# Nine key chunks for two heads, gate products between transposes and masks, and later expert weights, in a fused attention and expert kernel

## The chip, the cores and the metric

The kernel runs on one core of one Trainium2 chip. A core has five engines with queues of their own: TensorE (PE in the profile; its weight loads are listed apart as PEld), VectorE (DVE), ScalarE (ACT), GpSimd (POOL) and SyncE (SP), which here starts nearly all transfers. The metric is the device time of one execution in microseconds, as the median of several runs. Before the change it is 995.38 us (three runs, 995.27 to 997.89).

## The reference

Two stages. The first is attention with a top-32 mask in 64 pairs of batch and head, each with 576 queries and keys of 64 elements. The second sends every token to its best of eight experts, and each expert keeps only its 80 tokens of highest gate.

```python
# q, k, v: (8, 8, 576, 64); w_gate (512, 8); w1 (8, 512, 1024); w2 (8, 1024, 512); capacity 80
scores = scale * q @ k.T
kth = np.partition(scores, -32, axis=-1)[..., -32:-31]
attn = softmax of scores where scores >= kth, else 0          # row sums + 1e-9
x = (attn @ v) as (4608, 512)                                 # heads side by side

logits = x @ w_gate
expert_idx, gate_w = argmax and its softmax probability
for e in range(8):
    tok_idx = the tokens of e, at most the 80 with the largest gate_w
    out[tok_idx] = gate_w[tok_idx, None] * (np.maximum(x[tok_idx] @ w1[e], 0) @ w2[e])
# all other rows of out are 0
```

## The kernel before

The attention works on 32 head pairs n. Each has five tiles t of 128 queries: four with both heads, and a short one that holds the last 64 queries of both heads on one tile. A unit is one tile of one head (the short tile is one unit), so a pair has nine units, 288 in all, and one step of the program's loop brings one new unit into a software pipeline. For a unit, VectorE finds the 32nd largest score: MAX8 over six pieces of 96 columns, three rounds over the 48 candidates, a count of how many scores exceed a pivot (ScalarE, `sign`), and a last MAX8 over `y`, the scores multiplied by their signs.

```python
for j in range(NG):                                # 6 pieces
    nc.vector.max(out=cand[:, j, :], in_=s[:, j * S // NG : (j + 1) * S // NG])      # L241
# ... cut: three rounds of max and match_replace on cand (L252, L260)
nc.scalar.activation(sign, s, Act.Sign, bias=w9[:, 7:8], scale=-1.0, accum_out=cnt)  # L257
engine = nc.gpsimd if i in self.odd else nc.vector
engine.tensor_tensor(out=y, in0=s, in1=sign, op=Alu.mult)                            # L264
nc.vector.max(out=w9[:, 8:], in_=y)                                                  # L266
# ... cut: pick writes the threshold thr[:, i] (L269)
```

Then the scores that fall below the threshold are masked. `below` makes a mask per unit: 1 on GpSimd (even units), or the distance below the threshold on ScalarE (odd units). `turn_w` transposes the scores by chunks of 128 keys on TensorE, and adds the transposed mask with a large negative factor in the same PSUM accumulation, so that exp makes it 0. 576 keys are four chunks and a half, and each head takes five: the last one starts 64 keys early, so it overlaps the fourth, and its first 64 rows meet zeros in v.

```python
def turn_w(self, n, t):
    # ... cut: ab holds 2 heads x 4 chunks in PSUM, cc the last chunks, the products with v and the sums
    keys = [slice(c * P, c * P + P) for c in range(NF)] + [slice(S - P, S)]
    dst = [[ab[:, h, c, :] for c in range(NF)] + [cc[:, h * P : (h + 1) * P]] for h in range(g)]
    for h in range(g):
        sc = self.s.pop(i + h)
        for c in range(NK):                                                          # L316
            nc.tensor.matmul(dst[h][c], lhsT=sc[:, keys[c]], rhs=ident, ..., is_transpose=True)
    for h in range(g):
        mk = self.mask.pop(i + h)
        for c in (NF, *range(NF)):                                                   # L321
            nc.tensor.matmul(dst[h][c], lhsT=mk[:, keys[c]], rhs=huge if i + h in self.odd else minus, ...)
    nc.scalar.activation(wT[:, 2 * NF : ...], cc[:, : g * P], Act.Exp, scale=scale / TINY)   # L323
    nc.scalar.activation(wT[:, : g * NF, :], ab..., Act.Exp, scale=scale / TINY)             # L325
```

`back` multiplies these weights with v and a column of ones (L336, forty half-width products a full tile), `over` takes the reciprocal of the sums on VectorE (L348), `divide` scales on ScalarE (L359). When a pair is done, `norm` stores it, transposes it (L201), copies it as xT (L376), multiplies it with the gate's weights (L381) and copies the product (`part`, L388), each part in some later step:

```python
def norm(...):
    # ... cut: store xn
    yield 1
    ps = self.four()...; self.turn_in(ps, xn, cs); nc.scalar.copy(xT[:, at], ps[:, at])
    yield 1
    lp = self.four()...                   # the one PSUM buffer that front and turn use too
    for c in cs:
        for r in range(0, P, TL):
            nc.tensor.matmul(lp[r : r + TL, c, :], lhsT=xT[...], rhs=wg[:, hp, :], start=True, stop=True)
    nc.scalar.copy(part, lp[:, cs])
    yield 0
    # ... cut: VectorE adds part to lg (L392); after every eighth pair the gates
```

A part that ends before `yield 1` takes a step in which no `front` is due, since both need the one buffer. `front` (L226) makes the scores of the tile four units ahead, and ScalarE copies them to SBUF (L233).

Of the 4.2 MB of weights of each expert, four experts' are loaded during the attention. The fifth's are loaded when the attention's buffers are free, and those of experts 5 to 7 as the first ones' buffers come free. In the last stage the routing finds the kept tokens (mostly VectorE), GpSimd gathers their rows by an indirect transfer, and TensorE computes the experts.

```python
def finish(wpool, full):
    late = stack.enter_context(tc.tile_pool(name="late", bufs=1))
    for dma in load_w(4, late):
        dma()
    # ... cut: routing, gathers, hidden(e), product(e), store(e); load_w(e + 4, wpool) for 5 to 7
wpool = main.enter_context(tc.tile_pool(name="wpool", bufs=4))
for e in range(4):
    slow += load_w(e, wpool, 4)          # issued one by one in the attention's steps
```

Of the kernel before, what the change touches and what calls it, by code (L numbers as in the profile page):

```python
# [22 lines left out]
HUGE = 2.0 ** 100  # L23
TINY = 2.0 ** -48
# [3 lines left out]
def kernel(  # L28
# [120 lines left out]
    class Attention:  # L149


        def __init__(self, stack, lean):
# [6 lines left out]
            self.s, self.top, self.cnt, self.y, self.mask, self.w, self.xn = ({} for _ in range(7))  # L159
            self.thr, self.z = thr_all, z_all  # L160
# [4 lines left out]
            for j in range(1 if lean else 3):  # L165
                t = vpool.tile([P, NK, 2, D + 1], F32, name=f"vb{j}")
                nc.gpsimd.memset(t[:, :, :, D : D + 1], 1.0)
                nc.gpsimd.memset(t[: P - TL, NF, :, :], 0.0)
                self.vb.append(t)
# [4 lines left out]
        def load(self, n, b, hp):  # L174
            one = bass.ds(b, 1)
            tiles = []
            for name, src in (("qn", q), ("kn", k)):
# [7 lines left out]
                tiles.append(t)  # L185
            t = self.vb[n % len(self.vb)]
            for h in range(2):
                nc.sync.dma_start(
                    t[:, :NF, h, :D], v[one, 2 * hp + h, : NF * P, :].rearrange("o (c p) d -> p (o c) d", p=P))
            nc.sync.dma_start(  # L190
                t[P - TL :, NF, :, :D], v[one, 2 * hp : 2 * hp + 2, NF * P :, :].rearrange("o h p d -> p (o h) d"))
            self.qk[n] = tiles
# [23 lines left out]
        def front(self, n, t):  # L216
# [11 lines left out]
            s = self.rows.tile([P, 2 * S], F32, name="s", tag="s", bufs=2 if self.lean else 5)  # L228
            for h in range(g):
                self.s[i + h] = s[:, h * S : (h + 1) * S]  # L230
# [41 lines left out]

        def below(self, i):

            self.top.pop(i)
            self.mask[i] = self.rows.tile([P, S], BF16, name="mask", tag="mask", bufs=3)
            if i in self.odd:
                nc.scalar.activation(self.mask[i], self.s[i], Act.Relu, bias=self.thr[:, i : i + 1], scale=-1.0)  # L278
                return
            nc.gpsimd.tensor_scalar(self.mask[i], self.s[i], self.thr[:, i : i + 1], None, op0=Alu.is_lt)  # L280
# [13 lines left out]
        def drop(self, i):  # L294

            s, top = self.s[i], self.top.pop(i)
            self.mask[i] = self.rows.tile([P, S], BF16, name="mask", tag="mask", bufs=2)
            nc.vector.tensor_scalar(self.mask[i], s, self.thr[:, i : i + 1], top[:, 0, 0:1], op0=Alu.is_lt, op1=Alu.add)

        def turn_w(self, n, t):  # L300
# [9 lines left out]
            keys = [slice(c * P, c * P + P) for c in range(NF)] + [slice(S - P, S)]  # L310
            dst = [[ab[:, h, c, :] for c in range(NF)] + [cc[:, h * P : (h + 1) * P]] for h in range(g)]

            for h in range(g):
                sc = self.s.pop(i + h)
                for c in range(NK):
                    nc.tensor.matmul(dst[h][c], lhsT=sc[:, keys[c]], rhs=ident, start=c == 0 or (c == NF and h == 0), stop=False,  # L316
                                     is_transpose=True, skip_group_check=True)
            for h in range(g):
                mk = self.mask.pop(i + h)
                for c in (NF, *range(NF)):  # L320
                    nc.tensor.matmul(dst[h][c], lhsT=mk[:, keys[c]], rhs=huge if i + h in self.odd else minus, start=False, stop=True, skip_group_check=True)  # L321
            wT = self.rows.tile([P, 2 * NK, P], F32, name="wT", tag="wT")
            nc.scalar.activation(wT[:, 2 * NF : 2 * NF + g, :].rearrange("p h r -> p (h r)"), cc[:, : g * P], Act.Exp,  # L323
                                 scale=scale / TINY)
# [590 lines left out]
```

## Time and profile before

| | before |
|---|---|
| median of three runs | 995.38 us |
| span of the profiled execution | 993.1 us |
| attention, to the last gate sums | about 870 us |
| routing, gathers and experts | about 124 us |
| ScalarE busy, GpSimd busy | 797.2 us, 451.9 us |
| HBM read, written | 63.19 MB, 20.19 MB |
| two head pairs in mid-attention (the products with v at 365.47 and 417.64 us) | 52.17 us |

Engine rows give busy time, share of the span and number of instructions. The slices are fortieths of the span, 24.8 us each, with the busy share in tenths. A group line names its line of the program, the engine and operation, what is written and read with shapes, the number of instructions, and then busy us and mean ns of one, followed by the engine's idle time just before them and what ended it. Durations of neighbouring matmuls overlap in such a mean. A line of the waits says who waited for whom: us in total, how many times, and the longest.

### The profile page before, as it was taken

To read this page: it belongs to the slowest core of one execution; us is meant where nothing else is said; L and a number is where in the kernel's file an instruction comes from. 1 tells how busy PE (TensorE), PEld (TensorE's weight loads), DVE (VectorE), ACT (ScalarE), POOL (GpSimd) and SP (SyncE) were. 2 spreads that over 40 slices of the span, in tenths; PEclk is the share of its full clock that TensorE was granted. 3 is DMA by queue.
4 is the path that set the end of the run, shared out by engine and by line. 5 is a ranking of instruction groups with operands and counts; after the bars stand their busy time and mean duration, and the time that the engine had idled before them with its cause. 6 is when DMAs were issued, how large, how long until landed. Compare 5 with 4: busy or idle time off the path is not lost.

```text
span 993.1 us, 35590 instructions
## 1 busy us (share of the span) xinstructions
PE 885.5 (89%) x13368; PEld 704.9 (71%) x13368; DVE 870.6 (88%) x5072; ACT 797.2 (80%) x1652; POOL 451.9 (46%) x330
## 2 busy tenths in 40 slices
PE   5899999998989989899899999999899898679996
PEld 3677777776767777677677777777677676668896
DVE  5899999999999999999999999999999999571110
ACT  3899999999999989999999999999899999601110
POOL 2445555555455545554555555555455555302111
PEclk9999999999999999999999999999999999979998
DMA  3344453333332323333333322222222100044920
GB/s 72 97 126 131 129 134 92 92 92 92 91 79 62 87 82 86 92 92 93 88 82 83 91 49 51 50 50 50 50 50 49 41 23 14 16 170 142 382 76 28
DMA packets 167893, 85.76 MB, mean 86 GB/s; under 512 B 117792, under 2 KB 154656, under 8 KB 167712
## 3 DMA queue, kind: packets, MB, share of 16 engines
q1 hardware_dynamic: 166688, 80.78, 29.7%
q0 software_dynamic: 1024, 2.62, 0.9%
q8 instruction: 107, 1.75, 0.7%
q14 instruction: 74, 0.61, 0.2%
HBM read 63.19 MB, written 20.19 MB: 84 GB/s over the span
## 4 chain that ended last, share of the span: by engine, by line
DVE 53%; PE 24%; ACT 18%; issue 5%; DMA 1%; POOL 0%; POOLq 0%; SPq 0%; ACTq 0%; DVEq 0%
DVE cand L241 17%; DVE w L266 12%; DVE cand L260 6%; DVE y L264 6%; ACT s L233 4%; DVE top L252 4%; PE yp L799 4%; ACT wT L325 3%; PE sp L201 3%; PE cc L336 3%; ACT sign L257 3%; DVE pick L269 3%; ACT mask L278 2%; PE sp L226 2%; PE ab L316 2%
## 5 line engine op out<-in xcount | busy, mean ns | idle before, releaser
L241 DVE MAX8 cand<-s 128x8 f32<-128x96 f32 x1728 | 393.9, 250 | 8.9 <-ACT s L233 8.8
L280 POOL TENSOR_SCALAR mask<-s,thr_all 128x576 bf16<-128x576 f32 x144 | 248.2, 1723 | 144.9 <-DVE pick L269 121.8
L264 POOL TENSOR_TENSOR y<-s,sign 128x576 f32<-128x576 f32 x144 | 184.8, 1283 | 277.3 <-DVE pick L269 128.0
L336 PEld LDWEIGHTS cc<-vb,wT 128*64 128x64 f32 x5760 | 181.7, 138 | 111.2 <-ACT wT L325 98.5
L257 ACT ACTIVATE sign<-s,w 128x576 bf16<-128x576 f32 x288 | 225.4, 783 | 22.8 <-DVE w L252 22.2
L336 PE MATMUL cc<-vb,wT 128*64 128x65 f32 x5760 | 204.0, 225 | 40.6 <-ACT wT L325 38.9
L266 DVE MAX8 w<-y 128x8 f32<-128x576 f32 x288 | 217.8, 756 | 2.5 <-POOL y L264 2.5
L226 PE MATMUL sp<-both 64*128 64x288 f32 (+1 forms) x1280 | 202.1, 435 | 15.0 <-ACT part L388 6.5
L233 ACT ACTIVATE s<-sp 128x1152 f32<-128x1152 f32 (+1 forms) x161 | 167.3, 1040 | 12.7 <-PE sp L226 11.9
L316 PE MATMUL ab<-ident,s 128*128 128x128 f32 x1148 | 175.6, 282 | 0.0
L325 ACT ACTIVATE wT<-ab 128x1024 f32<-128x1024 f32 (+1 forms) x159 | 148.8, 936 | 0.0
L226 PEld LDWEIGHTS sp<-both 64*128 64x128 f32 (+1 forms) x1280 | 105.6, 179 | 53.8 <-ACT part L388 8.5
L316 PEld LDWEIGHTS ab<-ident,s 128*128 128x128 f32 x1148 | 127.5, 141 | 11.6 <-issue 0.9
L321 PEld LDWEIGHTS <-mask 128*128 128x128 bf16 x1440 | 92.1, 98 | 42.4 <-ACT mask L278 19.6
L252 DVE MAX8 top<-cand 128x8 f32<-128x48 f32 x576 | 116.9, 203 | 0.0
L260 DVE MATCH_REPLACE8 cand<-top,cand 128x48 f32<-128x48 f32 x576 | 112.9, 196 | 0.0
L278 ACT ACTIVATE mask<-s,thr_all 128x576 bf16<-128x576 f32 x144 | 112.3, 780 | 0.4
L264 DVE TENSOR_TENSOR y<-s,sign 128x576 f32<-128x576 f32 x144 | 107.6, 747 | 4.5 <-ACT sign L257 4.5
L359 ACT ACTIVATE xn<-cc,z_all 128x64 f32<-128x64 f32 (+1 forms) x320 | 86.5, 318 | 1.4 <-DVE z_all L348 0.8
L316 PE MATMUL cc<-ident,s 128*128 128x128 f32 x288 | 78.9, 274 | 0.3 <-ACT xn L359 0.2
L269 DVE SCALAR_TENSOR_TENSOR pick<-past,cnt,w 128x9 f32<-128x9 f32 x288 | 69.5, 241 | 0.2 <-DVE z_all L348 0.2
L323 ACT ACTIVATE wT<-cc 128x256 f32<-128x256 f32 (+1 forms) x160 | 56.2, 351 | 12.0 <-PE cc L321 11.3
(188 smaller groups left out, 965.7 us busy)
## 6 DMA issues: line engine op xcount, KB each, us to landing
w<-in_moe_w_dram SPq DMA_DIRECT2D x32, 512.0 KB, 4.7
w<-in_moe_w_dram SPq DMA_DIRECT2D x8, 2048.0 KB, 9.8
out_dram<-zero SPq DMA_DIRECT2D x9, 1024.0 KB, 6.3
qn<-in_q_dram SPq DMA_DIRECT2D x64, 128.0 KB, 2.6
kn<-in_k_dram SPq DMA_DIRECT2D x64, 128.0 KB, 2.5
vb<-in_v_dram SPq DMA_DIRECT2D x64, 128.0 KB, 2.6
xd<-xn SPq DMA_DIRECT2D x32, 256.0 KB, 4.3
qn<-in_q_dram SPq DMA_DIRECT2D x32, 32.0 KB, 2.5
```

The lines of the kernel that those rows point to most:

```text
L226: nc.tensor.matmul(o, lhsT=qT[d, t * P : t * P + m], rhs=kT[d, j * HS : (j + 1) * HS], start=True, stop=True)
L233: nc.scalar.activation(s[:, j * HS : (j + w) * HS].rearrange("p (j c) -> p j c", c=HS), ps[:, j : j + w, :HS], Act.Copy, scale=TINY)
L241: nc.vector.max(out=cand[:, j, :], in_=s[:, j * S // NG : (j + 1) * S // NG])
L252: nc.vector.max(out=dst, in_=cand)
L257: nc.scalar.activation(sign, s, Act.Sign, bias=w9[:, 7:8], scale=-1.0, accum_out=cnt)
L260: nc.vector.match_replace(out=cand, in_to_replace=dst, in_values=cand, imm_value=LOW)
L264: engine.tensor_tensor(out=y, in0=s, in1=sign, op=Alu.mult)
L266: nc.vector.max(out=w9[:, 8:], in_=y)
L280: nc.gpsimd.tensor_scalar(self.mask[i], self.s[i], self.thr[:, i : i + 1], None, op0=Alu.is_lt)
L316: nc.tensor.matmul(dst[h][c], lhsT=sc[:, keys[c]], rhs=ident, start=c == 0 or (c == NF and h == 0), stop=False, is_transpose=True, skip_gr ...
L325: nc.scalar.activation(wT[:, : g * NF, :], ab.rearrange("p h c r -> p (h c) r")[:, : g * NF, :], Act.Exp, scale=scale / TINY)
L336: nc.tensor.matmul(cc[r : r + TL, o], lhsT=wT[:, h * NF + c if c < NF else 2 * NF + h, r : r + TL], rhs=vb[:, c, h if t < NF else r // TL, ...
```

## The change

A tile's two heads lie side by side, 1152 score columns in all, which are exactly nine chunks of 128. The change transposes and masks these nine, where each head had five; the middle chunk holds the last 64 keys of head 0 and the first 64 of head 1. For that, v is laid out anew: four chunks of head 0, four of head 1 that start at its key 64, four of head 1 from its key 0 (for the short tile, which still has five chunks), and four single chunks padded with zeros. Head 1's v is so loaded twice. The mask of both heads lies in one tile, and one factor (`huge`, now 2^80) serves both kinds of mask, since a chunk may hold both.

```diff
-                t = vpool.tile([P, NK, 2, D + 1], F32, name=f"vb{j}")
+                t = vpool.tile([P, 3 * NF + 4, D + 1], F32, name=f"vb{j}")
...
+        def load_v(self, n, b, hp):
+            for j, h, k0 in ((0, 0, 0), (1, 1, TL), (2, 1, 0)):
+                nc.sync.dma_start(t[:, j * NF : (j + 1) * NF, :D], v[one, 2 * hp + h, k0 : k0 + NF * P, :]...)
+            # ... two loads of 64 rows, one of 64 rows of both heads; called one unit pair after load
...
-            self.mask[i] = self.rows.tile([P, S], BF16, name="mask", tag="mask", bufs=3)
+                self.mask[n, u // 2] = self.rows.tile([P, 2 * S], BF16, name="mask", tag="mask", bufs=2 if self.lean else 3)
...
-        def turn_w(self, n, t):
+        def turn_w(self, n, t, between=None):
...
+            keys = [slice(c * P, c * P + P) for c in range(2 * NF + 1)] if t < NF else [...]
+            for c, o in enumerate(dst):
+                nc.tensor.matmul(o, lhsT=sc[:, keys[c]], rhs=ident, ..., is_transpose=True)
+            if between:
+                between()
+            for c in sorted(range(len(dst)), key=lambda c: c != NF):
+                nc.tensor.matmul(dst[c], lhsT=mk[:, keys[c]], rhs=minus if self.lean else huge, ...)
+            wT = self.rows.tile([P, 2 * NF + 1, P], F32, name="wT", tag="wT")
+            nc.scalar.activation(wT[:, 2 * NF, :], cc[:, :P], Act.Exp, scale=scale / TINY)
```

The gate's products of a pair no longer wait for a step without a front. They go into the next tile's `turn_w`, after its transposes and before its masks, where TensorE may have to wait for the masks:

```diff
             nc.scalar.copy(xT[:, at], ps[:, at])
-            yield 1
+            yield 2
...
+                def gate():
+                    for g in later:
+                        if ready[g] == 2:
+                            ready[g] = next(g)
...
-                    self.turn_w(*units[i - 4][:2])
+                    self.turn_w(*units[i - 4][:2], gate)
...
-                    if ready[g] and busy and not last:
+                    if (ready[g] == 1 and busy or ready[g] == 2 and i < NU + 4) and not last:
```

The larger v and mask tiles need room. Three experts' weights are loaded during the attention and not four, and those of experts 3 and 4 at the start of the last stage:

```diff
-        late = stack.enter_context(tc.tile_pool(name="late", bufs=1))
-        for dma in load_w(4, late):
-            dma()
+        late = stack.enter_context(tc.tile_pool(name="late", bufs=2))
+        for e in (3, 4):
+            for dma in load_w(e, late):
+                dma()
...
-        wpool = main.enter_context(tc.tile_pool(name="wpool", bufs=4))
-        for e in range(4):
+        wpool = main.enter_context(tc.tile_pool(name="wpool", bufs=3))
+        for e in range(3):
             slow += load_w(e, wpool, 4)
```

## The prediction

> **What bounds the kernel now.** I read first the page's busy shares and slices, to see which engine is full and when.
>
> ```profile
> PE 885.5 (89%) x13368; PEld 704.9 (71%) x13368; DVE 870.6 (88%) x5072; ACT 797.2 (80%) x1652; POOL 451.9 (46%) x330
> ...
> PE   5899999998989989899899999999899898679996
> ...
> DVE  5899999999999999999999999999999999571110
> ```
>
> Over the whole span TensorE and VectorE look equally full, 89% and 88%. The slices separate them: VectorE is full up to slice 34 (about 860 us) and nearly idle in the last five, where TensorE goes on with the experts. So there are two stages, and the attention stage must be read by itself. The windows do that (columns: busy us and instructions of PE, PEld, DVE, ACT, POOL; granted clock; DMA share; GB/s).
>
> ```profile
> 200.00:300.00 100.00, 90.45 (x1307) 70.66 (x1303) 99.27 (x591) 91.88 (x191) 50.51 (x35) 1.00 0.34 91
> ...
> 700.00:800.00 100.00, 91.51 (x1325) 71.36 (x1323) 99.31 (x592) 93.39 (x195) 51.66 (x35) 1.00 0.21 50
> ```
>
> VectorE is busy 99.3 of every 100 us, TensorE 91. VectorE's total over the attention is the time. I then asked for the waits, to see what VectorE still loses:
>
> ```profile
> PE cc L321 <- POOL mask L280: 13.7, 32, 1.5
> ...
> ACT wT L323 <- PE cc L321: 11.3, 18, 2.0
> PE cc L321 <- ACT mask L278: 10.5, 30, 0.4
> ...
> DVE y L264 <- ACT sign L257: 4.5, 13, 0.4
> ```
>
> The multiplication y waits for ScalarE's sign 13 times, 4.5 us in all; restricted to 100 to 840 us it is 3.7 us in 11 waits. Between 40 and 855 us VectorE's timeline has no other wait over 0.3 us. TensorE waits for masks and ScalarE for TensorE, but these lie inside slack that VectorE does not see.
>
> Last, is VectorE's busy time real, or stretched by a neighbour? The instructions of line 264 on VectorE, from 100 to 840 us (min/median/max ns):
>
> ```profile
> L264 DVE TENSOR_TENSOR y<-s,sign x127: 735/747/759, 101.3 to 837.4; 128x576 f32<-128x576 f32 x127
> ```
>
> 735 to 759 ns is a spread of 3%: nothing stretches it that the change could relieve.
>
> **What the Trainium skill says.** "Perfetto Trace Analysis", section Identifying Performance Opportunities: improving a kernel generally means improving its most-contended engine. By occupancy that is VectorE here, in 34 of 40 slices. "SBUF — State Buffer", section Who interferes with whom: DMA does not contend with compute engines, while a VectorE operation with two SBUF inputs contends with a GpSimd one that reads. The first half agrees: DMA share 0.34 and 0.21 in the two windows above, VectorE 99.27 and 99.31. The second is not visible: GpSimd is half busy and y keeps to 735 to 759 ns. "TensorE: Matmul & The Clock Gate", section Back-to-back issue gap: a stream of weight loads and 128-wide matmuls runs at about 81 ns each. Here the timeline has four transposes from 303.22 to 303.65 us, 108 ns each in fp32, and four bf16 mask products from 319.37 to 319.59, 55 ns each. The measured spacings are used, not the 282 and 220 ns of the group means, which overlap.
>
> **The change part by part.**
>
> *Nine chunks in place of ten.* In a tile of 128 queries and two heads, one fp32 transpose and one mask product go: 0.108 + 0.055 to 0.06 = 0.17 us of TensorE. There are 128 such tiles (32 head pairs by 4), so 128 x 0.17 = 21.6 us of TensorE. The exp of the small buffer shrinks from 128x256 to 128x128 (367 and 288 ns in the groups by shape): 128 x 0.079 = 10 us of ScalarE. The forty half-width products with v stay. On VectorE nothing goes: it keeps the same instructions, in the same order except for the few additions of the gate's sums, which move ahead by some steps. So of 31.7 us saved on two engines, none is in VectorE's sum of 99.3%. What can come through is at most the 3.7 us of waits for the sign: ScalarE is 92 to 93% busy and slightly earlier in each tile. These waits sit in one kind of step only, where three ScalarE operations queue (mask, sign, sign, at 322.84 to 324.94 us), and the freed 0.08 us per tile covers a part. I take 1.5 of 3.7 us.
>
> *Gate products between transposes and masks.* They are 20 records, 0.76 us at 315.27, once per head pair, in the step of the short tile, which has one unit's time and not two. The page has the front of that step waiting 6.5 us in total for ScalarE's copy of them. They go to a full tile's step, where the transposes end at 303.76 us, xT has been copied by 303.37, and ScalarE is busy with a sign until 304.74 us. The products would run 303.76 to 304.5 and their 0.2 us copy comes just when ScalarE is free. The masks then move back by 0.76 - 0.11 = 0.65 us, to about 305.0, and the large exp wanted to start at 305.0. So ScalarE loses 0.1 to 0.2 us in this step and wins as much in the short one. Net for VectorE: 0.
>
> *Masks in one tile of both heads, three buffers.* Twice the room; GpSimd's few waits for TensorE (about 19 us, lines 201 and 321) may shorten. GpSimd is 46% busy: 0.
>
> *v loaded again.* Six transfers for three, 448 for 288 KB a pair. The DMA share is 0.2 to 0.4 and the data are used two pairs (52 us) later: 0. At the start, the second pair's q and k are issued some 1.8 us later, at about 8 to 12 us, and needed at 22.4: 0.
>
> *Drain.* After VectorE's search ends near 857 us the chain is serial through TensorE and ScalarE for two full tiles: 2 x (0.17 + 0.10 for exp) = 0.55 us saved. The last gate products but one only change places with transposes.
>
> *Weights of experts 3 and 4 at the end.* Now only expert 4 comes here, from 869.3 us:
>
> ```profile
> 870.00:875.00 5.00, 1.01 (x6) 0.58 (x6) 3.50 (x16) 0.27 (x1) 0.57 (x3) 0.50 0.90 313
> 875.00:880.00 5.00, 4.13 (x46) 3.27 (x47) 4.76 (x17) 0.00 (x0) 0.00 (x0) 0.50 1.01 388
> 880.00:885.00 5.00, 5.00 (x38) 4.13 (x37) 4.72 (x13) 0.00 (x0) 0.00 (x0) 0.80 0.36 138
> ...
> 890.00:895.00 5.00, 4.97 (x59) 4.39 (x59) 1.50 (x8) 0.00 (x0) 0.00 (x0) 1.00 0.00 0
> ```
>
> 4.2 MB take until 883 us at up to 388 GB/s. Another 4.2 MB need 10.8 us more and end near 894 us. Expert 3's hidden layer starts at 926.7 us: over 30 us of slack. In the chain in order of time the first gather of token rows starts at 897.59 us and takes 3.10 us. "DMA: Bandwidth & Descriptors", section Issuing engines are not separate DMA queues, says that all transfers interleave on the same 16 engines, so an overlap would lengthen it; the gap is 3 us. I put 0.2 us here.
>
> Sum: -1.5 - 0.55 + 0.2 = -1.9 us, or 993.5 from 995.38 us.
>
> **The rivals.** *TensorE is the true bound.* For it: 91% busy, and 24% of the chain runs through it. Then most of 21.6 us comes out, 974 us. Against: VectorE's 99.3% leaves under 1 us in 100 to anything else. *The inserted gate products delay masks, exp and the next signs.* If all 0.76 us of each of 32 pairs came out, 24 us, about 1018. For it: ScalarE at 93% has little to catch up with, and y waits for sign already. Against: the front is four steps, some 11 us, ahead of its use, and the times above fit to 0.2 us. A partial form, 0.1 us a pair, would take 3 us and cancel the gain. *The late weights run into the gather or a wait.* If the loads begin 2 to 3 us later, because their room lies under other attention tiles, they reach 897 us and the gather of 3.1 us takes perhaps 5 to 6: 2 to 3 us lost, about 996. *The start.* Some 5 us of VectorE waits lie before 37 us, where TensorE is slower (2.3 us for eight products of the front, 1.2 us later); part of them could go: 1 us at most.
>
> **Range and chances.** The parts are small: 0 to 3.7 us won in the body, 0.5 in the drain, up to 3 lost at the end or by shifted signs; the three times before spread by 2.6 us. That gives 990 to 996.8. Two per cent are 20 us: faster needs the first rival (0.03), slower the second in full or something unseen in the last stage (0.02).
>
> **What would show it.** VectorE at 99% in the same windows with its sum unchanged (870 us); TensorE's busy time lower by 20 us and more, LDWEIGHTS too, and idle time in its place; the wait of y for sign below 4.5 us; no wait of the front for ScalarE's copy of the gate products; DMA full from 870 to about 894 us and the gather still near 3.1 us. I am wrong if VectorE's busy share in the body falls, if its instructions become shorter, or if the last stage (869 us to the end, 124 us) changes by more than 2 us.

## The result, and the profile after

| | before | after |
|---|---|---|
| median of four runs beside each other | 996.48 us (995.27 to 997.89) | 989.66 us (988.02 to 992.00) |
| span of the profiled execution | 993.1 us | 986.1 us |
| attention, to the start of the last addition to lg | 869.47 us | 858.40 us |
| from there to the end | 123.6 us | 127.75 us |

The ratio is 0.9933, with an interval of 0.9906 to 0.9959: 6.8 us less, where 1.9 us were predicted. The time is 0.3 us below the range. The table shows that this is a difference of two errors: the attention gained about 11 us in this pair of traces (1.5 + 0.55 were predicted), and the last stage lost 4.1 us (0.2 were predicted).

Three rows of the page of after, engine busy times and the slices:

```profile
PE 865.1 (88%) x13112; PEld 679.3 (69%) x13112; DVE 866.3 (88%) x5072; ACT 786.7 (80%) x1652; POOL 451.9 (46%) x333
...
PE   5898989898898998998889898988898898699896
...
DVE  5999999999999999999999999999999999561110
```

TensorE lost 20.4 us of busy time and 256 instructions, as worked out (128 tiles, two instructions each). VectorE kept its 5072 instructions and still lost 4.3 us of busy time. It should have lost none, and that is the first sign of what the prediction missed (3.1 us of it lie in the line of `pick`, which comes up below). The same windows as before, in the same columns (busy us and instructions of PE, PEld, DVE, ACT, POOL; clock; DMA share; GB/s):

```profile
200.00:300.00 100.00, 88.60 (x1278) 68.17 (x1278) 99.83 (x603) 92.55 (x194) 51.79 (x35) 1.00 0.36 98
700.00:800.00 100.00, 90.19 (x1298) 69.52 (x1295) 100.00 (x595) 93.14 (x197) 52.77 (x35) 1.00 0.21 50
```

VectorE went from 99.27 and 99.31 to 99.83 and 100.00, and the two windows together hold 1198 instructions where they held 1183: 1.3% more, with 0.6% more busy time. The waits that the busy share shows are gone, and more came out than they held. The waits of after (who waited for whom: us in total, times, longest):

```profile
PE cc L340 <- ACT mask L294: 29.0, 40, 0.8
PE cc L340 <- POOL mask L296: 26.3, 20, 1.6
...
ACT wT L343 <- PE cc L340: 3.0, 2, 1.8
...
DVE y L273 <- ACT sign L266: 0.8, 2, 0.4
```

TensorE, with less to do, waits more for masks (10.5 and 13.7 us before). The exp of the small buffer waits 3.0 us for TensorE and not 11.3, and y for its sign 0.8 us and not 4.5. The wait of the front for `part` (6.5 us before) is not in the list any more.

**Two waits in a pair, one of them hidden.** Nine units make a pair and the engines' roles alternate from unit to unit, so every second pair has GpSimd's y where its neighbour has VectorE's. In what follows the pairs are numbered from 0. The mean lengths of a pair, from its first MAX8 on `cand` to that of the next pair, are 25.78 us before and 25.25 after for the odd pairs from 3 on, 26.79 and 26.73 for the even ones. The 15 odd pairs from 1 to 29 sum to 7.7 us less, the 15 even pairs from 2 to 30 to 0.9 us less. So the gain sits in one kind of pair. Aligning the VectorE instructions of pair 11 in both traces, the start times drift apart at two places. The first, in before (timeline, lines of one stretch: start, length, engine, operation; idle time ahead of it in brackets):

```profile
315.27 0.76 PE L381 MATMUL sp<-wg,xT 128*64 128x8 f32 x20
...
316.31 1.19 PE L226 MATMUL sp<-both 64*64 64x288 f32 x8 [0.29 <-ACT part L388]
...
319.59 0.22 PE L321 MATMUL cc<-minus,mask 128*128 128x128 bf16 x1
...
319.85 0.39 ACT L323 ACTIVATE wT<-cc 128x256 f32<-128x256 f32 x1 [0.46 <-PE cc L321]
...
321.68 1.13 ACT L233 ACTIVATE s<-sp 128x1152 f32<-128x1152 f32 x1
...
322.84 0.78 ACT L278 ACTIVATE mask<-s,thr_all 128x576 bf16<-128x576 f32 x1
...
323.52 0.76 ACT L257 ACTIVATE sign<-s,w 128x576 bf16<-128x576 f32 x1
...
324.40 0.76 DVE L264 TENSOR_TENSOR y<-s,sign 128x576 f32<-128x576 f32 x1 [0.34 <-ACT sign L257]
```

The gate products and the copy of them hold the front by 0.76 + 0.29 us; TensorE is so late with the next tile's last mask for the small buffer that the exp waits 0.46 us; ScalarE then has no idle time until the sign, and y waits. In after the gate products are not in this stretch, the small buffer's mask product stands first of the nine (314.37), and ScalarE runs from 314.14 us to the sign without a wait:

```profile
314.14 0.78 ACT L266 ACTIVATE sign<-s,w 128x576 bf16<-128x576 f32 x1
314.80 0.21 ACT L266 ACTIVATION_READ_ACCUMULATOR sign<-s,w 128x1 f32 x1
314.89 0.28 ACT L343 ACTIVATE wT<-cc 128x128 f32<-128x128 f32 x1
...
318.48 0.76 ACT L266 ACTIVATE sign<-s,w 128x576 bf16<-128x576 f32 x1
```

Counted from the last MAX8 on a GpSimd y before it (316.50 and 312.41 us), the sign starts after 7.02 us before and 6.07 us after. The wait needed 0.42 us, so it vanished. I call it the wait for the sign.

The second place is ahead of that MAX8. There no view shows a wait at all. The lines of `pick` on VectorE between 100 and 840 us (min/median/max ns), in before and in after:

```profile
L269 DVE SCALAR_TENSOR_TENSOR pick<-past,cnt,w x253: 205/214/669, 102.7 to 839.0; 128x9 f32<-128x9 f32 x127
```

```profile
L278 DVE SCALAR_TENSOR_TENSOR pick<-past,cnt,w x256: 202/213/529, 101.5 to 837.2; 128x9 f32<-128x9 f32 x128
```

In the records of before, 239 of the 253 picks take 205 to 232 ns and the other 14 take 492 to 669. An operation on nine columns that takes 214 ns and now and then 669 is probably not working in the rest. In pair 11 of before:

```profile
313.21 1.15 ACT L233 ACTIVATE s<-sp 128x1152 f32<-128x1152 f32 x1
...
314.22 0.80 ACT L257 ACTIVATE sign<-s,w 128x576 bf16<-128x576 f32 x1
...
315.19 1.28 POOL L264 TENSOR_TENSOR y<-s,sign 128x576 f32<-128x576 f32 x1 [2.91 <-DVE cand L241]
...
315.84 0.65 DVE L269 SCALAR_TENSOR_TENSOR pick<-past,cnt,w 128x9 f32<-128x9 f32 x1
...
316.42 0.08 DVE L269 DVE_READ_ACCUMULATOR pick<-past,cnt,w 128x1 f32 x1
316.50 0.76 DVE L266 MAX8 w<-y 128x8 f32<-128x576 f32 x1
```

GpSimd's y ends at 315.19 + 1.28 = 316.47, and the pick, started at 315.84, ends at 316.49. The MAX8 after it needs that y. So it looks as if the wait for GpSimd's y is booked as the length of the instruction ahead of it; kernel 15 below tests that. And GpSimd's y itself starts 0.09 us after ScalarE's sign has been read out (the read ends at 315.10), though the view names `cand` as its releaser, and the sign stands in ScalarE's queue behind the copy of the next tile's scores. I call this the hidden wait. In after the same lines stand at:

```profile
309.12 1.14 ACT L242 ACTIVATE s<-sp 128x1152 f32<-128x1152 f32 x1
...
310.13 0.79 ACT L266 ACTIVATE sign<-s,w 128x576 bf16<-128x576 f32 x1
...
311.10 1.28 POOL L273 TENSOR_TENSOR y<-s,sign 128x576 f32<-128x576 f32 x1 [2.78 <-ACT sign L266]
...
311.89 0.51 DVE L278 SCALAR_TENSOR_TENSOR pick<-past,cnt,w 128x9 f32<-128x9 f32 x1
```

0.65 became 0.51 us. Some 0.08 us of that can be the smaller exp, which stands ahead of the copy in ScalarE's queue, with the large exp and the division between them (from its start to that of the copy 1.57 us before, 1.49 after).

Both waits can be summed from the records: for the wait for the sign, the start of y less the start of the MAX8 ahead of it, less the normal 160 ns; for the hidden one, what each pick has over 214 ns. Over the sixteen odd pairs, before: 4.7 and 7.5 us. After: 0.0 and 4.5 us. The difference is 7.8 us. Over the fifteen of them whose length was summed above it is 7.7 us, which is the whole change of the odd pairs. The rest of the 11 us is in the first pair (28.63 and 27.33 us) and the last one (41.77 and 40.54 us to the last addition). Those vary by as much in traces of one kernel: in the repeat of after below they are 28.24 and 41.89 us, and in kernel 7 below, which has the attention of before, 27.48 and 40.73 us. So 8.6 us in the body are the firm part.

### The profile page after: what moved, and what is told of

The parts are those of the page before. It is cut to its first block, busy times and chain, and to the rows that moved or that the text cites. A ratio compares the mean times of both kernels' runs of the same rounds, so it can differ in the third digit from the quotient of the medians.

```text
span 986.1 us, 35265 instructions
## 1 busy us (share of the span) xinstructions
PE 865.1 (88%) x13112; PEld 679.3 (69%) x13112; DVE 866.3 (88%) x5072; ACT 786.7 (80%) x1652; POOL 451.9 (46%) x333
## 3 DMA queue, kind: packets, MB, share of 16 engines
q1 hardware_dynamic: 188608, 86.03, 31.5%
## 4 chain that ended last, share of the span: by engine, by line
DVE 59%; PE 29%; ACT 7%; issue 3%; POOL 1%; DMA 1%; SPq 0%; POOLq 0%; ACTq 0%; DVEq 0%
DVE cand L250 19%; DVE w L275 14%; DVE cand L269 7%; DVE y L273 7%; PE cc L357 6%; PE sp L234 4%; DVE top L261 4%; PE yp L830 4%; PE sp L209 4%; DVE pick L278 3%; DVE w L261 2%; PE ab L334 2%; ACT wT L344 2%; ACT mask L294 1%; PE ab L340 1%
## 5 line engine op out<-in xcount | busy, mean ns | idle before, releaser
L250 DVE MAX8 cand<-s 128x8 f32<-128x96 f32 x1728 | 389.6, 246 | 9.1 <-ACT s L242 8.9
L266 ACT ACTIVATE sign<-s,w 128x576 bf16<-128x576 f32 x288 | 224.9, 781 | 29.6 <-DVE w L261 27.3
L242 ACT ACTIVATE s<-sp 128x1152 f32<-128x1152 f32 (+1 forms) x161 | 167.6, 1042 | 10.5 <-PE sp L234 9.8
L340 PEld LDWEIGHTS <-mask 128*128 128x128 bf16 x1312 | 76.9, 97 | 79.1 <-issue 37.3
L340 PE MATMUL ab<-huge,mask 128*128 128x128 bf16 x1148 | 89.9, 219 | 0.0
L340 PE MATMUL cc<-huge,mask 128*128 128x128 bf16 x160 | 35.7, 223 | 58.9 <-ACT mask L294 29.0
L278 DVE SCALAR_TENSOR_TENSOR pick<-past,cnt,w 128x9 f32<-128x9 f32 x288 | 66.4, 230 | 0.2 <-DVE z_all L369 0.2
```

The lines of the kernel that those rows point to most:

```text
L340: nc.tensor.matmul(dst[c], lhsT=mk[:, keys[c]], rhs=minus if self.lean else huge, start=False, stop=True, skip_group_check=True)
```

## The experiments

Waits are in us over the sixteen odd pairs, computed as above; "even" is added where there is something in the even pairs from 2 on. Waits and stages are those of one trace for each kernel. The last stage is split at the first matmul of a hidden layer (to hp, from hp on). The ratio is to before, timed beside it on the same chip (medians of before: 995.4 to 996.5 us).

| kernel | median | ratio (95%) | for sign | hidden | attention ends | to hp | from hp on |
|---|---|---|---|---|---|---|---|
| before | 996.48 | | 4.7 | 7.5 | 869.5 | 31.7 | 91.9 |
| after | 989.66 | 0.9933 (0.9906 to 0.9959) | 0.0 | 4.5 | 858.4 | 32.8 | 95.0 |
| 1 gate products moved, alone | 993.65 | 0.9966 (0.9955 to 0.9977) | 0.3, even 0.9 | 7.6 | 867.2 | 31.7 | 93.1 |
| 2 after without that move | 993.92 | 0.9974 (0.9963 to 0.9985) | 2.4 | 4.6 | 864.9 | 32.9 | 95.0 |
| 3 late weights, alone | 998.39 | 1.0016 (1.0004 to 1.0029) | 4.6 | 7.2 | 867.2 | 34.8 | 95.0 |
| 4 after, again | 989.53 | 0.9926 (0.9906 to 0.9946) | 0.0 | 4.5 | 860.7 | 33.1 | 94.9 |
| 5 half of expert 3 early | 989.20 | 0.9933 (0.9914 to 0.9951) | | | 861.3 | 33.3 | 94.3 |
| 6 after, no refills | 987.54 | 0.9912 (0.9888 to 0.9936) | | | 861.0 | 33.1 | 91.6 |
| 7 before, no refills | 994.63 | 0.9987 (0.9972 to 1.0001) | | | 867.6 | 31.5 | 91.4 |
| 8 tenth chunk, mask last | 1004.07 | 1.0083 (1.0062 to 1.0103) | 0.4, even 6.7 | 10.3 | 873.1 | 34.3 | 95.6 |
| 9 middle chunk's mask last | 989.44 | 0.9941 (0.9925 to 0.9956) | 0.0, even 0.4 | 5.9 | 861.3 | 34.3 | 91.3 |
| 10 tenth chunk, mask early | 992.35 | 0.9968 (0.9958 to 0.9978) | 0.0, even 1.3 | 6.9 | 862.9 | 33.2 | 94.4 |
| 11 kernel 1, small masks first | 993.35 | 0.9976 (0.9966 to 0.9985) | 0.0, even 2.4 | 8.5 | 867.8 | 32.5 | 92.4 |
| 12 before, padded by 85 | 998.55 | 1.0027 (1.0017 to 1.0037) | | | 867.8 | 33.3 | 96.4 |
| 13 after, padded by 85 | 987.83 | 0.9909 (0.9892 to 0.9925) | | | 860.7 | 33.1 | 94.1 |
| 14 after, padded by 40 | 990.81 | 0.9947 (0.9930 to 0.9964) | | | 858.4 | 32.9 | 95.4 |
| 15 after, sign ahead of the copy | 986.79 | 0.9901 (0.9886 to 0.9917) | 0.0 | 0.1 | 856.6 | 34.5 | 95.0 |

### The parts alone (1 to 4)

Kernel 1 is before with the move of the gate products only, kernel 2 is after with that move undone, kernel 3 is before with the weights of experts 3 and 4 loaded late.

```diff
# 1: before, with
+            if between:
+                between()                       # in turn_w, after the transposes
-            yield 1
+            yield 2
-                    self.turn_w(*units[i - 4][:2])
+                    self.turn_w(*units[i - 4][:2], gate)
# 2: after, with these three put back
# 3: before, with
-        late = ...tile_pool(name="late", bufs=1)
-        for dma in load_w(4, late):
+        late = ...tile_pool(name="late", bufs=2)
+        for e in (3, 4):                        # and wpool with 3 buffers for 3 experts
```

> The kernel before with the gate products alone moved into the next full tile's step; ten chunks and four early experts stay. Theory A (the attention's 11 us come from freeing the short tile's step of these products): the pair with the wait loses its 0.6 us, the attention ends 8 to 10 us earlier, total about 986 to 988 us, below the changed kernel, since the late weights are not there. Theory B (they come from the shorter transposes, masks and exp): 0 to 2 us, about 994 to 996 us.

> The changed kernel with the gate products put back into a step without a front. Theory A: 1 to 3 us of the attention's gain stay and the last stage keeps its 4 us loss, 996 to 998 us. Theory B: 8 to 10 us of the gain stay, about 990 to 991 us.

> The kernel before with experts 3 and 4 loaded at the start of the last stage. Theory C (the late weights cost the 4 us of the last stage: full DMA, slower supply of TensorE's instructions): last stage 127 to 128 us and total 998 to 1000 us. Theory D (the 4 us come from where TensorE's instruction fetches and clock steps fall, not from the weights): last stage within 1.5 us of 123.6 us, total 994 to 997 us.

> The changed kernel once more, beside the others. All theories: 989 to 990 us. Its second trace shows how much of the last stage's 127.7 us repeats: theory C 127 to 128.5 us, theory D may show 125 to 128 us.

The move alone takes 0.34% off, though it was expected at net 0 in the prediction, and what it cuts is the wait for the sign alone: 4.7 to 0.3 us, with 0.9 us new in the even pairs. The hidden wait kept its sum (7.6 us). Its longest pick even grew, for which I have no shown cause; over 100 to 840 us of kernel 1:

```profile
L269 DVE SCALAR_TENSOR_TENSOR pick<-past,cnt,w x255: 201/214/876, 100.1 to 838.8; 128x9 f32<-128x9 f32 x128
```

Nine chunks without the move halve the wait for the sign (4.7 to 2.4) and cut the hidden one (7.5 to 4.6). Together they leave 0.0 and 4.5. The pairs 1 to 30 are shorter by 3.0 us in kernel 1, by 5.1 us in kernel 2 and by 8.6 us in after, so the two parts nearly add. Kernel 3 takes nothing from the attention's pairs and costs 0.16% (0.04 to 0.29): the late weights, in this form, are a small loss. The repeat of after gives the same body and the same last stage as the first.

### Is it TensorE's work or the order of the masks (8 to 11)

Kernel 8 adds to after the tenth transpose and mask product of a full tile again, into columns that nothing reads; its mask comes last. Kernel 10 is the same with that mask right after the middle one. Kernel 9 has no more work, but the middle chunk's mask last of nine. Kernel 11 is kernel 1 with the small buffer's masks of both heads first.

```diff
# 8: after, with
+            if t < NF:
+                nc.tensor.matmul(cc[:, 384:512], lhsT=sc[:, keys[0]], rhs=ident, ..., is_transpose=True)
...              # after the nine masks (10: right after the middle chunk's mask)
+            if t < NF:
+                nc.tensor.matmul(cc[:, 384:512], lhsT=mk[:, keys[0]], rhs=huge, ...)
# 9: after, with
-            for c in sorted(range(len(dst)), key=lambda c: c != NF):
+            for c in sorted(range(len(dst)), key=lambda c: c == NF):
# 11: kernel 1, with
-            for h in range(g):
-                for c in (NF, *range(NF)):
+            for h, c in [(h, NF) for h in range(g)] + [(h, c) for h in range(g) for c in range(NF)]:
```

> The changed kernel with the tenth chunk's transpose and mask product put back on TensorE in each full tile, into a part of the small buffer that nobody reads; exp stays at 128x128. If the chunks help through TensorE's 0.17 us per tile, the waits of VectorE come back in part: attention 3 to 5 us longer, total 992 to 994 us, about the kernel before with the gate products moved alone. If they help through ScalarE's exp, shorter by 0.08 us, total 989.5 to 990.5 us.

> The changed kernel with the middle chunk's mask product last in each tile instead of first; no work is added. Theory O (what counts is when the small buffer is complete, since ScalarE's queue stands still until its exp can start): ScalarE's wait for the small buffer rises from 3 us to 20 us and more, the attention gets 8 to 14 us longer, total 998 to 1003 us. Theory W (what counts is TensorE's work of 0.17 us per tile): no change, 989 to 990.5 us.

> The tenth chunk's TensorE work put back as in the run before it, but its mask product right after the middle chunk's, so the small buffer is complete almost as early as in the changed kernel. Theory O: the attention gets 0 to 3 us longer, total 989.5 to 992.5 us. Theory W: as long as with the product at the end, about 1003 us.

> The kernel before with the gate products moved, and both heads' small-buffer masks taken first (ten chunks, early weights). Theory O: the small buffer is complete 0.2 us earlier than with the gate products alone, the attention 2 to 4 us shorter than there, total 990 to 992 us. Theory W: no gain over the gate products alone, 993 to 994.5 us, or a loss where the first mask product now waits for both heads' masks.

The same added work on TensorE, which is not the bound, lengthens pairs 1 to 30 by 14.1 us in kernel 8 and by 4.0 us in kernel 10 (by medians to kernel 4 it is 14.5 and 2.8 us). The mask's place alone (kernel 9) costs 1.9 us there; its equal total has a shorter last stage in it. In the form with ten chunks (kernel 11) the place gains nothing either. So neither of the two theories, order and work, holds by itself: kernel 9 speaks against the order alone (998 us and more were expected), kernel 10 against the work alone (about 1003). In kernel 9 ScalarE's wait for the small buffer rises from 3.0 to 14.0 us, and little of it reaches VectorE. And in kernel 10, which keeps the small exp, the hidden wait is 6.9 us and not 4.5, so the smaller exp alone does not hold the gain. Two lines of the waits of kernel 8:

```profile
ACT wT L349 <- PE cc L346: 24.1, 64, 2.3
...
DVE y L273 <- ACT sign L266: 6.1, 17, 0.4
```

The exp waits for the tenth mask 64 times, and that reaches VectorE: the sum of both waits in all pairs but the first is 17.4 us, against 4.5 in after; the difference, 12.9, is most of the 14.1 us. By the spacings of the prediction (108 ns a transpose, 55 a mask product) the small exp is held back by an estimated 0.4 us in kernel 9, 0.2 in kernel 10 and 0.6 in kernel 8. That fits a slack of a few tenths of a microsecond a tile in ScalarE's queue, with little cost inside it and much beyond. It is argued and not shown, and it can't be one threshold, since kernel 10 delays the small exp less than kernel 9 and costs more. That before stood just past such a slack would explain why TensorE's saved time came through at all.

### The hidden wait, by itself (15)

If the pick's extra length is the wait for GpSimd's y, and that the wait for a sign behind the copy of the scores, then the copy put behind the sign must take it out. It is done in one of 18 steps, the one where the wait sits; nothing else is changed.

```diff
+                copy = lambda j=j, w=w: nc.scalar.activation(s[...], ps[...], Act.Copy, scale=TINY)
+                if hold is None:
+                    copy()
+                else:
+                    hold.append(copy)           # issued right after the next sign
-                    self.front(*units[f][:2])
+                    self.front(*units[f][:2], held if i % 18 == 11 else None)
```

> The changed kernel with one ScalarE copy of scores in every second head pair put behind the sign that follows it, so this sign starts up to 0.8 us earlier. If the part of pick's length over 214 ns is VectorE's wait for GpSimd's y, and this waits for the sign in ScalarE's queue, that part falls from 5 us to 1 to 2 us in all and the attention ends 3 to 4 us earlier, total 986 to 987 us. If pick is long for another reason, no change or a loss where the held copy delays the next front: 989 to 992 us.

In the same stretch of pair 11 the sign is now ahead of the copy, GpSimd's y ends at 311.29 and the pick is short:

```profile
309.05 0.78 ACT L270 ACTIVATE sign<-s,w 128x576 bf16<-128x576 f32 x1
...
309.81 1.14 ACT L242 ACTIVATE s<-sp 128x1152 f32<-128x1152 f32 x1
...
310.01 1.28 POOL L277 TENSOR_TENSOR y<-s,sign 128x576 f32<-128x576 f32 x1 [1.76 <-DVE cand L273]
...
311.81 0.21 DVE L282 SCALAR_TENSOR_TENSOR pick<-past,cnt,w 128x9 f32<-128x9 f32 x1
```

From 100 to 840 us:

```profile
L282 DVE SCALAR_TENSOR_TENSOR pick<-past,cnt,w x258: 201/213/221, 102.6 to 839.8; 128x9 f32<-128x9 f32 x129
```

The longest pick is 221 ns. The hidden wait falls from 4.5 to 0.1 us, the odd pairs by 0.29 us each, and the time to 986.79 us, 0.9901 of before (0.9886 to 0.9917). By medians it is 2.9 us below after, the lowest of all kernels here. The hidden wait is shown by this, and with it that VectorE's busy time contained one.

### The last stage (3, 5 to 7, 12 to 14)

Kernel 5 loads half of expert 3's weights (w1) during the attention again. Kernels 6 and 7 are after and before without the refills: experts 5, 6 and 7 compute with the weights of 0, 1 and 2, and their loads are left out. Kernels 12 to 14 only put small matmuls of one zero column (85, 85 and 40) at the start of the program, whose result nothing reads; they move all that follows in TensorE's program.

```diff
# 5: after, with
+        w3pool = ...; slow += load_w(3, w3pool, 4, which="1")
-            for dma in load_w(e, late):
+            for dma in load_w(e, pool, which="2" if e == 3 else "12"):
# 6, 7: after, before, with
-                        for dma in load_w(e + 4, wpool):
-                            dma()
+                        w1_t[e + 4], w2_t[e + 4] = w1_t[e - 1], w2_t[e - 1]
# 12 to 14: before, after, after, with
+                for _ in range(85):             # 14: 40
+                    nc.tensor.matmul(pad[:, 0, :1], lhsT=z[:, :P], rhs=z[:, :1], start=True, stop=True)
```

> The changed kernel with the first weights of expert 3 (2.1 MB) loaded during the attention again, into the 16 KB per partition that are left there. Theory C (each late megabyte lengthens the last stage): half of the extra 4.2 MB goes, so the stage from the first hidden layer to the end falls from 94.9 to about 93.5 us and the total to about 988.5 us. Theory D (only where instruction fetches fall): no trend, 989 to 990 us.

> The changed kernel without the loads of experts 5 to 7, which use the weights of experts 0 to 2 instead (this leaves out 12.6 MB of loads; the output of these experts is another). If TensorE's issue gaps of 4 to 5 us are instruction fetches behind a full DMA, they go, and the stage from the first hidden layer to the end is 90 to 90.5 us, total about 985 us. If they come from the program's layout alone, they stay and it is 94.9 us, total 989.5 us.

> The kernel before without the loads of experts 5 to 7, which use the weights of experts 0 to 2. Fetches behind a full DMA: its 2.5 us of issue gaps go too, the stage from the first hidden layer to the end is 89.5 to 90.5 us like that of the changed kernel without these loads, total about 994 us. Layout alone: 91.9 us, total 996 us.

> The kernel before with the same 85 matmuls. Theory D: the stage from the first hidden layer to the end leaves its 91.9 us, to 93 to 95 us. Theory C: it stays at 91.5 to 93 us, as in the three kernels with early weights.

> The changed kernel with 85 one-column matmuls of zeros put ahead of its first transpose, which shift every later instruction fetch of TensorE by about half of a fetched block. Theory D (where the fetches fall decides the issue gaps): the stage from the first hidden layer to the end leaves 94.9 us, to 91 to 93.5 us. Theory C (the late weights decide): it stays at 94.5 to 95.5 us. Total plus up to 1 us from the start.

> The changed kernel with 40 such matmuls, about a quarter of a block. Theory D: the stage from the first hidden layer to the end lies anywhere from 91 to 95 us, differing from the run with 85. Theory C: 94.5 to 95.5 us.

The loads did what was predicted: in after they fill DMA from 863 to 884 us, and the gather on the chain, at 887.72 us, takes 2.88 us. (The prediction calls its counterpart at 897.59 us the first gather; it is the second one issued.) Half of the weights back early (5) changes little: 94.3 us from hp on. Still the last stage is 4.1 us longer, in two places.

*From hp on, 3.1 us.* TensorE stands still for no wait that the profile names. Its timeline in after, among the second, third and fourth expert:

```profile
915.32 2.20 PE L830 MATMUL yp<-hT,w 128*64 128x80 f32 x51 [0.59 <-issue]
...
921.62 2.17 PE L815 MATMUL hp__17329<-xt,w 128*64 128x80 f32 x57 [1.03 <-issue]
...
927.61 2.44 PE L830 MATMUL yp<-hT,w 128*64 128x80 f32 x61 [0.76 <-issue]
...
939.84 2.70 PE L830 MATMUL yp<-hT,w 128*64 128x80 f32 x70 [1.23 <-issue]
```

The DMA records have transfers of 16 KB in the queue of instructions (q8), and TensorE resumes 1.4 to 1.5 us after one of them has landed (at 913.95, 920.2, 926.2 and 938.4 us for these four). That the queue is TensorE's is inferred: its 105 transfers for 26,224 matmuls and weight loads are 250 of these to a transfer. Meanwhile the refills keep DMA full, 1.03 of its time at 358 to 416 GB/s in the windows of 5 us from 910 to 930 us. Idle times over 150 ns from hp on, less one of 0.58 at the last store that all kernels have, sum to 2.5 us in before and 4.6 in after, which is 2.1 of the 3.1 us; the rest is not located. Without the refills they are 1.8 and 1.9 us and the stage is equal, 91.6 and 91.4 us (6, 7). So the loss needs the refills. But it isn't bound to the late weights. Kernel 12 has before's loads, and nothing but 85 tiny matmuls at the start:

```profile
930.83 1.20 PE L788 MATMUL hp__17672<-xt,w 128*64 128x80 f32 x29 [1.10 <-issue]
937.09 3.60 PE L803 MATMUL yp<-hT,w 128*64 128x80 f32 x97 [1.04 <-issue]
...
950.16 3.95 PE L803 MATMUL yp<-hT,w 128*64 128x80 f32 x106 [1.78 <-issue]
```

Its stage from hp on is 96.4 us and not 91.9, with 6.1 us of such idle time, and kernel 9, with late weights, has 91.3. Neither expectation for it reached that. The total confirms the direction: 2.6 us by medians. Yet the same padding moves after by 0.9 us down (13), and 40 matmuls by 0.4 us up (14). So a change of the program's layout alone can move this stage by 4.5 us; that it does so through where the instruction transfers fall against the refills fits the traces, but is argued. Of the kernels with late weights and refills all but kernel 9 lie between 94.1 and 95.6 us, and those with early weights at 91.9, 92.4, 93.1 and, kernel 12, 96.4. Whether that is chance of placement or something in the late loads stays open.

*To hp, 1.1 us.* One part, 0.6 us, is the clock. The 48 products `acc` of the routing run in before from 891.77 us, in after from 880.44. Windows of 2 us, before and then after (the clock is the number ahead of the last two):

```profile
892.00:894.00 2.00, 2.00 (x31) 2.00 (x30) 0.00 (x0) 0.00 (x0) 0.00 (x0) 1.00 0.00 0
894.00:896.00 2.00, 2.00 (x26) 1.89 (x25) 0.51 (x4) 0.00 (x0) 0.00 (x0) 0.92 0.00 0
```

```profile
882.00:884.00 2.00, 2.00 (x25) 2.00 (x24) 0.00 (x0) 0.00 (x0) 0.00 (x0) 0.78 0.99 380
884.00:886.00 2.00, 2.00 (x13) 1.62 (x13) 0.57 (x4) 0.00 (x0) 0.00 (x0) 0.50 0.03 13
```

In after the clock fell to half inside the products, at 883.10 us; in before it fell at 895.66, after the last of them. From the first of the 48 to the last it takes 3.39 us before and 4.03 after, 5.82 in kernel 3 and 5.72 in kernel 15, where the clock fell still earlier. The end of the attention sets when the routing starts, and the clock changes at times of its own, so this is spread that a single trace can't assign to the change.

The other part is no spread. The chain in order of time (start, length), before and then after, from the indices of the rows (`idx_x`) to the first gather that GpSimd issues:

```profile
895.63 0.17 DVE idx_x L751
...
896.09 0.35 POOL xg L761
```

```profile
885.01 0.18 DVE idx_x L782
...
885.30 0.68 issue
...
886.23 0.35 POOL xg L792
```

From the end of `idx_x` to the gather it is 0.30 us before and 1.05 us after. All kernels with early weights have 0.30 (before, 1, 7, 11, 12), and all with late ones 1.05, or 0.96 in kernel 5. Kernel 3, whose late weights are its only change, has 1.05 too. So about 0.75 us of the loss comes with the late weights in this form. In it GpSimd waits for nothing that the profile names, and why stays open. Against these two parts, the products start 0.3 us sooner after the attention.

## Why the prediction was wrong

- **VectorE is the bound, TensorE's 20 us stay off the path:** right. PE fell from 885.5 to 865.1 us and VectorE filled to 99.8 and 100.0. The first rival, 974 us, is out.
- **"I take 1.5 of 3.7 us":** the first term that failed. The place was right, exactly the step named (mask, sign, sign at 322.84 to 324.94 us), but the whole wait went: 4.7 us, not 1.5. What was wrong is what feeds it. The prediction gave the 0.08 us of the exp and put ScalarE's waits for TensorE "inside slack that VectorE does not see". One of these, 0.46 us at 319.85 us, stands ahead of the sign in ScalarE's queue. The gate products' move alone takes the wait for the sign to 0.3 us, nine chunks without it to 2.4. Its size was low too: the idle time printed is counted from the end of the instruction ahead, which overlaps its successor, so 0.34 us printed are 0.42 us in the starts.
- **"nothing stretches it":** the step that failed in kind. It was tested on y alone, 735 to 759 ns. The line of `pick`, 205/214/669 ns, shows the stretch. It held 7.5 us of the hidden wait, and 3.1 of them went; the prediction had named shorter instructions as a sign of being wrong. With the term above that is 7.8 us where 1.5 stood, which is most of the attention's error. The busy share of 99.3% was taken as work; after kernel 15 we know that some 1% of the body's busy time was waiting.
- **"Net for VectorE: 0" for the gate products:** failed. Alone the move takes 0.34% off: the step that they leave had no slack (4.7 us of waits for the sign became 0.3), and the step that they go to gave back little. The second rival, that they delay masks and signs, shows only with ten chunks, as 0.9 us in the even pairs of kernel 1 and 2.4 in those of kernel 11.
- **The exp, 0.08 us a tile:** right in size (0.367 us in before, 0.269 in the mean of after's, and 0.08 us between the starts around it), and it is a part of what reaches the hidden wait. The sum of 10 us over all tiles said nothing of where it counts; two steps in each odd pair decide, and kernel 10 shows that the exp alone is not enough there.
- **Drain, 0.55 us:** not shown. From the last pair's start to the last addition, 41.8 us before, 40.5 after and 41.9 in its repeat.
- **Start, under 1 us:** not shown either; the first pair has 28.6, 27.3 and 28.2 us in the same three traces.
- **Late weights, 0.2 us:** the reasoning on loads and the gather's length held (DMA full to 884 us, gather 2.88 us), and the last stage still lost 4.1 us. The third rival named the wrong collision: the gather is not longer, it is issued 0.75 us later. Another 0.6 us is the clock, and 3.1 us are lost from hp on, for which waits of TensorE's own instructions under full DMA are argued and whose tie to the late weights is open. The prediction said that a change of over 2 us there would prove it wrong, and it did.
- **The range:** its lower end let the body win at most 3.7 us, the sum of one line of the waits. That bound was no bound, since the view only showed waits that are not booked as busy.

What is not closed: the body's 8.6 us and the last stage's 4.1 would make 4.5 us, and the medians differ by 6.8. The first pair and the last account for the other 2.5 us in these two traces, but they differ by 2.2 us between two traces of after as well, and untraced runs can't be split.

The Trainium skill, "TensorE: Matmul & The Clock Gate", section Architectural detail, says that ScalarE's queue is strictly first in, first out. Both waits agree with it. In the hidden one a sign stands behind a copy (1.01 us from its start to the sign's), and kernel 15, with the two exchanged, has 0.0 and 0.1 us left of the two waits. In the other one the sign at 323.52 us comes behind an exp that waited 0.46 us for TensorE.

## What to carry to other kernels

An engine that is 99% busy can still be waiting: before taking its busy time as fixed, compare the shortest, median and longest duration of every one of its operations, the small ones first, and lay a long one beside what ends when it ends. Time saved on an engine that is not the bound is worth what it does to the few steps where the bound engine waits for a queue behind it, so follow those steps in the timeline and don't multiply by the number of tiles. And where a last stage is fed by transfers at full rate, a change of nothing but the program's layout can move it by several microseconds, as in kernel 12; repeat with padding before giving it a cause.

## What the runs showed of the hardware

- The wait of a VectorE instruction was booked as the length of the one before it: 214 ns of `pick` became up to 669 (before), and were 221 at most in kernel 15, where what the next instruction waits for came earlier.
- The queue of instructions moved transfers of 16 KB, and under DMA at 1.03 of its time TensorE stood idle four times in after, for 0.59 to 1.23 us, and resumed 1.4 to 1.5 us after such a transfer had landed. 85 one-column matmuls at the start of the program lengthened a stage 900 us later by 4.5 us in one trace each, and the whole by 2.6 us in medians.
- In the clock records of the traces, the full clock in the last stage lasted 13.65 us after its rise, four times 3.413 us, and then it was half for 3.4 to 10.2 us; the products of 16 columns went from 72 to 134 ns apart. The Trainium skill, "TensorE: Matmul & The Clock Gate", section What's actually happening, has a window of 3413 ns that runs freely, which agrees; the rise came 12.5, 11.0, 9.2 and 10.6 us after the last addition in before, after, kernel 3 and kernel 4.
- The median duration of VectorE's MAX8 on `cand` was between 245 and 251 ns in different traces, without order by kernel, while two in a row started 160 ns apart in each. A group's mean duration is no measure of its pace.
